# A fused attention and feed-forward kernel on one core: a new written-out instruction order and a constant tile set at the start

## The chip, the cores and the metric

One core of one Trainium2 chip runs the whole kernel; the other seven are idle. The metric is the device time of one execution in microseconds (us). The kernel before takes 803.41 us, the median of three runs (800.26, 803.41 and 803.42).

## What is computed

The reference runs three layers in a row. Attention has 2 batches, 8 heads, 768 positions and head size 64. Each position of q and k gets a 6-bit bucket from the signs of its product with `proj`, and a score counts only where the two buckets agree. Two feed-forward layers of 1536 tokens follow (512 to 2048 to 512):

```python
q_bits = (np.einsum('bhsd,dk->bhsk', q, proj) > 0)          # k_bits likewise
mask = q_bucket[:, :, :, None] == k_bucket[:, :, None, :]
scores = np.where(mask, scale * np.matmul(q, k.transpose(0, 1, 3, 2)), -1000000000.0)
attn = softmax(scores);  x = attn @ v
h = x @ w_in;   g = np.where(h >= 1, h, np.where(h <= -1, 0.0, (h + 1) ** 2 / 4));  x = g @ w_out
h = x @ w_in2;  g = h - np.tanh(h);                                                 return g @ w_out2
```

The four weight matrices arrive as 64-bit floats.

## The kernel before, in words

**Numbers as pairs.** TensorE multiplies in a format with fewer bits than float32, so each operand is kept as a high part and a low part (XH and XL, GH and GL, WH and WL, and so on), and a product is three matmuls: high by high, low by high, high by low. Making a pair takes a copy (`copy_hi`, line 235, the traced line is 236) on ScalarE or VectorE, and a subtraction (`sub_lo`, line 241), on GpSimd (traced as line 242) or VectorE (line 243).

**Attention.** A group is one head of one half of the query positions; it has three tiles of 128 queries, so there are 96 tiles. `prep_q`, `prep_k` and `first_k` make the pairs of q and k, and `q_bits` and `k_bits` multiply them by `proj` on TensorE and turn the signs into bucket rows on VectorE (lines 353 and 339). All results of these small products share the PSUM tile `pb`, and each of them must be read out by VectorE before the next is written. `emit_s` (lines 444 and 448) makes the scores of one tile; `soft` takes the maximum on VectorE (462), two small scalar steps (465), the exponential on ScalarE (466), and the high and low parts of the result (471 on ScalarE or VectorE, 472 on GpSimd or 473 on VectorE), which a transposing DMA on SP's queue turns around (477). `scale_l` prepares the division by the row sums (495, 499, 503) and `pv` multiplies by v (559). For three of the 16 pairs of heads `turn` transposes on TensorE instead (521, 529). `clear` (300 on ScalarE, 301 on GpSimd) writes zeros into the lower half of a pair's tile by scaling the identity matrix `unit`, which a DMA brings at the start.

**Feed-forward.** There are 128 units of 24 matmuls (`mats`, line 718), in six phases; a unit reads one or two blocks of weights. `w_narrow` turns a block of 64-bit weights into 32-bit ones (671 on ScalarE, 672, 673 and 675 on VectorE) and stores them for the second batch (679); `w_split` makes the pair. `post` evaluates the activation and adds up the outputs (737 to 768). The units of the first batch run between the attention tiles of the second half.

**Order.** Nothing loops on the chip. Python lists all steps as ops (`Plan.op`) with the cells they read and write, and a string, `SCHEDULE` (line 21), holds the order of the ops and, for each op that can run on more than one engine, which one runs it. `Plan.unpack` (line 96) reads it: three bytes an op, two for the place in the list of ops that are left, one for the engine. If the length does not fit or an op would come ahead of one that it depends on, the list's own order is used. Each engine then runs its ops strictly in the order of the string.

**The start and the spins.** Ahead of the ops a few lines are written out by hand (194 to 211). SP loads `proj` and the identity; VectorE sets constants, makes the pairs of `proj`, and at last copies the identity into `warm`:

```python
V.tensor_copy(warm, unit)        # line 211
def spin():                      # line 870
    for _ in range(4):
        T.matmul(WT, warm, warm, start=True, stop=True)
```

A spin is an op on TensorE whose product nobody reads; it keeps that engine active. There are 65, and the string places them like any other op (traced as line 872).

Of the kernel before, what the change touches and what calls it, by code (L numbers as in the profile page):

```python
# [20 lines left out]
SCHEDULE = (
    "c-rk)du)~E8GoMl@_p}jJKt%0F70VgdwMx-Y3cn!OE0ug5Gr+omWhs=8X&=V8JSClfCY3S0y+ehh{z=%x|<l83mGhIUXW-ci+51mqDz*|%s-4-X5yZ=OvQ5A"
    "o{Gub#uF&t_kPd&d!P6BT+9Bd90gV>x-OWe2@vFr#Xn<~qmCnhR7%{z{n{HG8^RW-L@ijVQUMq+&JIRou@3>BU+^hkJ-07D9UuT6WM{jPZp9dz)e3il!2<yh"
    "83hH^uJ9{Yun<7mzI{r6XN84^<M_Vs1QH3bqlotWP$2@&$;izOBId;7aaxPTY)8t>o4*r=o}Not8CfOq@3XGEzN4dKVjE&_?>f#;{{fgWsgW_Lt7~m-Mc@*q"
    "Pj{Okc6>^sgI!&dZ2NFW?ZS?ZB<p6ZxYJ~%rG>1eZX%Q*vb?;VERkD_<MTQ?V~IrKfxNsYlgVTwNpe+QUNP2K5FM``h(x2Mxhhmv7A`8TsK^e73Mwi9GPAO>"
    "jDn(!!t7`~uc9IzhlmL|;v>w=$a8rt*9l~2_XQm%9F9i&v$E=)42Ex1(k92U=w}w@x1Y!?b<i{&6_4BIZ*4QniXMrEVlhPHW8a8IeI{HXcrfVNwryGQ_>?ne"
    "EdIwGisz6#q!i$L_?mnbgBcL^*~=$gFXO|%y+R~gZ?acR&s)CSgTuJeF~PV(04TM@&+&6qL@6l^i%AJ^?X|A^){U&d;hY=HFhE|5NY5)dUjfk7)djatBEZR$"
    "+izTd@+6b+^2u%y3^p%byqG9#U~J*SmDmVN8Wz<!;BrUVSMJ%f2iR;@MreJ;Lq^|a;?!0#bITU-TKugzz$O8c5$`*Op4V~59UdOTyYBoI;<}b2M>x-{LX=Xj"
    "z*`k+`RVdqyK;B!`aYmxh+T*~$TY<Gb=yAsbQ@#$-pi0JWD5|lfx8gruEl4c?OgN0@7EkZj<TO__q*WpE4aV?*TC4}qel-NIz+MZ$tU>C$4@_f@F1E`y+`5y"
    "bMw@xQ<Ma6zWM(9^0C)Xp8;X-6K}t5oqhv|_m=?R#Yn_7Eel^faUu-cbjn2hc&?C+6h~DKDZnA)kRXN+W@cvUAP)rQ1p>kS-bdi?Wgoy_A@HXU{~QR|XPE1{"  # L30
    "?^^Ht<un6$=N-$+ef9MmMG_95)G#jzMybP}fBw1W=naoaOCAxXiI#yB-CRok6ylTOAD;jo#)C*{<Ue*G7Xtf%zV6xm>~8QLeRMYkC+!x(aLzc5_rrZe=w^95"
    "BSUg6C%|4?bhoy0m9cK6kq59{=r;yiwrtpdLOikqF%Y=>7Jn<-!q_7ZGQgia*ua-kfEcUxY^F?<13MY4-GNH2+I|~jLP~bk5BYL=i{#=a0es`300}`YUAh!)"
    "JH##P`u<6rlTT@P-=%g~R72JepthE{G+WEs$|jU`bSweUC?`xPSt!+P@||R?it;RmVTyy2l9J}4A|VoWbqgj>ork<8zp075dZiO1l~{6IcCA}p3=Sj`Av=*^"
    "mZ4^{DGdz`<SV0HAZBsiEPY>c^lOr?D+>w=cp@R}{5+v}EXIxcY{Ljs_yZk9>i_h^H8o*_gay4owc|JuKr1tcBg+lyWx9xA-b%H>3}RM<laZz=4Bw}kima}V"
    "g;{9s)mMjTqbj!z&N7ONi$O#a32AYF$=#V(vRG$lEY^-~Z3+XX5o!tv$C2Q(X+PsrNe4KY-rm)fB)=Cq%~au}EC>c!?W|3;m)`@>-{1dZ`b%kS2WHG*P=-!V"
    "k}6&Iwr<<^(Yp5rEo|8`p%{NsDWj=rpz-!KYvjPdfa}h;Ec@8ry)|IDa_7#Sp10!#Rd#H)G!+yd6^DPbY}w(WBLA7f!mS&*vGEtb^gO(4{S)gYP$Fd9!4&K?"
    "O$qKSd|Zgj_8&Ol;QsxTE(YAfmQi35L&z870si83_wQpbIGTq|KVrti*Wj(F>AU~n0Kk0|XzYm<_dE`Uv3}paBS#Q*HYmB{=>hYm?GKTF4X}bj33u-{_U_%h"
    "2XU9s!VLa!MDpzqz?Q8Bad2=mhmD)~#>Wo0F6Vo75wsXvvj*m55lLJ75w9o#^a~el*Z>K{e4TCv7^_!Xt5%uUOQ3{Ygp9ff;_4f5<ysGkriM9l=-u#5#7o&a"
    "A$oiFUL8b!8yGuKu&%DlIYh1r%nVSiW#}yV?riE(j?=ebK+c~(b0I7MF>fAxZ#uUxxp~@6jBz2J5X{b?;%WExavpBw^UNM#Qc)r^bN1}nbkP<eS}m(_#tcd%"
    "-v_9v!EPRbO4i;UV&$b&^_!Yd^HiV~m=rv1s@!NX?XE7PsS~lm1SAk4FYzRZDFPK1heDainp;|^Y*WxSH1MFy@-&6i!AgTc%d!k3zc!zc6|WeNszS%N@orKx"  # L40
    "c!^RxKR;jPR&`fZRiVX<aZ%Q&zt@3PSSZL@o|lD5CmZedcBYsMhHZP<*@lN)@XQ3EQ#24ZwF8zV1ic56fdVTiAQ;Ta<GF?riA0!b(w`upSpvl#_higLD;i}H"
    "A}O35iAE?Xi<6iMMMa6i5-N?Eh}0*YsOLDLZW0s-En21%5`!sIgqYSXdW7gi;=QA<5682K6QQrUrM$dsI>RokM*(x%IIq-o6(*F%lA@-jCI;k}Zq8xc`1bC("
    "6<2k6lPD<MmbU&30P<43UvE#HTCgY($elWM>a?oySJ`$&0Ooi!(EzwDI;?m@b#;sy#w5`tI{G@L%n~I+%qRw)&;_`oqq?)5SG85wRBQTpcek#B)zx)1t#k#Y"
    "nwxujVMe7nYgR$IoK}liJwsH{MLIhxD+N-C6{4i0zP_!^s&8!QYv}3esh?t5qPniWd$5cnwO%#}O6%&dzP`4$xwNT<^ZMq(!rF$)Lb_RFV>x5V(sAP|N-J5i"
    "jNquSl5=VHDJm%`Dk2QY;sv?%Au4i2gx<p<6eeMM?g-JS1G+a4W{?lmIvvX~4Bc}mEU3X{WVo(DvlulB(Ag}Id$!GV){=3=02KpG1kG#G)!E7{0@TIB(%(!$"
    "v{)8c)WNh!jlrq5Q)MM3WCmlNNA1D3IS*2^Wzw}AKx!|v?oq2mi&Gk!z-gaj(jFjSQs%_7<4~Xx9N{uWElKGSSn9s)lCeVgf;tzTEirl&0ZJi7wOyfQnFK)S"
    "O#4f5gZd9CNQ!8#1f?qXv~Mi*=xU6eJ&qdzs)S^nMPPJ_UZ>Vf&-5VlqYxCZlI}!LwoMELwHGx%N_SktJ&UCqj@~p#1_!F%Heph5GuoneGr^g5%b+$Htn&>}"
    "aBZSQZ8Br}j&u*&55&7pMj>eq^E?2?Q87<2NuDBikSQiLQK1Vr&5D{Gx~WJ00>LfXpok-ChBOh9S2;BWQ=6;D4#L;#WGvH7k*Yl%sSP7Ck%Jsm5lYgEkUC_@"
    "L?rHw!H^<Fb8rUKgPsXOPd4PF!Mx&{Uoq$%jZMVRJzz8$T|+CmUvuMdn?~8}4B6y3qiZ_p13Kp{IFKGfdImcwQJgVj<9P`7P!*lH`k$d+aAaIeL(?8%-G*;S"
    "Fs&t^Tpkv{N(*3YR^bq=&(rS9g`xI+Ge=uzk%nC9-?=@ys1%Q*?)?H?Y2CrMa}HFW|4?73oU1-8yc)rJ1^*?2-%_mqU6%e&DZD5b<)U1ai;{jTz_Vj4p1Uwq"  # L50
    "Ww@4s7jW*-BhuB!Zv|`Lm>HPHy>KLj)T4je<{^&FSvZQd_%$w%7Z^-<!It2EG?p&ZFg*X4tP4E_$7~1=4OdLZ*wI4jJS-d&Rp&qt8|XL|X3qJQ7Dr<WhfDBt"
    ">j$O?;xv;B$3z6CwKQB(A*B63A*r33DkyN&YBFkgUT~79wg5+De8?XBx(Ped)o^4yOqU8AbDv4Y0)EBGX&#vtA7h*>5XS0x9M$(@F1~5xXUcR&Oh1Nk4D$fu"
    "Xm`aiR{IeygNUii;dxfzuo;G5@gt@#Bg2*yOi_w)7{f8eOf+1d#MI8ik#jAT8*sEhfK;}BN#RgSQ*iMW=2K#g+QH6Wz+pmhxL${&x8AfS%nOr$0b~5bO#"
)


# [868 lines left out]
```

## Time and profile before

| | us |
|---|---|
| median of three runs | 803.41 |
| the profiled execution, own time | 806.18 |
| the profiled execution, span from first to last instruction | 804.4 |
| busy: TensorE matmul / VectorE / ScalarE / GpSimd | 755.5 / 607.2 / 461.8 / 307.5 |

The profiled execution is 2.77 us over the median, and 1.78 us of its time lie outside its span. A row of the trace names the engine (PE is TensorE's matmul, DVE VectorE, ACT ScalarE, POOL GpSimd, SPq SyncE's queue of DMA issues), the line, the operation, output<-inputs, shape and count. Square brackets hold the engine's idle time just ahead and what ended it.

### The profile page before, as it was taken

How to read it: one execution, taken by the hardware profiler on the slowest of the kernel's cores; microseconds unless marked ns; L12 is line 12 of the kernel's file. 1: busy time of each engine (PE TensorE's matmuls, PEld its weight loads, DVE VectorE, ACT ScalarE, POOL GpSimd, SP SyncE). 2: the span in 40 equal slices, each digit the busy share in tenths (PEclk: the TensorE clock that was granted, in tenths of full speed). 3: DMA queues.
4: the chain of work that ended last, by engine and by line, in shares of the span. 5: the costliest groups of instructions: out<-in, count | busy, mean ns of one | idle time of the engine just before them, and what ended most of it. 6: DMA issues, size and time to landing. Idle time of an engine off the chain costs nothing. (4 is left out here: it accounts for less than half of the span.)

```text
span 804.4 us, 12604 instructions
## 1 busy us (share of the span) xinstructions
PE 755.5 (94%) x4604; PEld 694.8 (86%) x4604; DVE 607.2 (75%) x1038; ACT 461.8 (57%) x747; POOL 307.5 (38%) x209
## 2 busy tenths in 40 slices
PE   5678999898899999998999999999999999999998
PEld 3557777777698899997999999989999999999997
DVE  7889988989898999999999998945444454444633
ACT  6778987977785778766865674524334132231220
POOL 6553254256444355533232554313131144202331
PEclk9999999999999999999999999999999999999999
DMA  5788696799967799397787788563221302121312
GB/s 183 144 197 207 178 233 184 205 227 240 210 182 179 187 220 225 108 215 208 195 201 215 194 193 206 160 137 125 66 66 53 92 27 79 59 74 52 92 40 79
DMA packets 163726, 123.38 MB, mean 153 GB/s; under 512 B 126800, under 2 KB 133712, under 8 KB 163664
## 3 DMA queue, kind: packets, MB, share of 16 engines
q1 hardware_dynamic: 163664, 122.58, 59.7%
q8 instruction: 36, 0.59, 0.3%
q14 instruction: 26, 0.21, 0.1%
HBM read 71.96 MB, written 19.92 MB: 114 GB/s over the span
## 5 line engine op out<-in xcount | busy, mean ns | idle before, releaser
L242 POOL TENSOR_TENSOR wl<-wr,wh 128x512 fp32r<-128x512 f32 x87 | 119.0, 1372 | 253.7 <-ACT wh L236 151.3
L718 PE MATMUL mm<-xh,wh 128*128 128x384 f32 x512 | 137.5, 339 | 2.3 <-DVE tmp L739 1.3
L718 PE MATMUL mm<-gh,wh 128*128 128x384 f32 x512 | 137.1, 338 | 2.1 <-DVE tmp L739 1.6
L718 PE MATMUL mm<-xh,wl 128*128 128x384 f32 x512 | 136.0, 336 | 0.4 <-POOL wl L242 0.4
L718 PE MATMUL mm<-gh,wl 128*128 128x384 f32 x512 | 135.6, 335 | 0.1
L718 PE MATMUL mm<-gl,wh 128*128 128x384 f32 x512 | 135.6, 335 | 0.1
L718 PE MATMUL mm<-xl,wh 128*128 128x384 f32 x512 | 135.6, 335 | 0.0
L472 POOL TENSOR_TENSOR phl<-p,phl 128x768 f16<-128x768 f32 x46 | 79.1, 1719 | 89.5 <-ACT phl L471 73.5
L236 ACT ACTIVATE wh<-wr 128x512 fp32r<-128x512 f32 x98 | 60.7, 623 | 83.5 <-PE mm L718 70.7
L466 ACT ACTIVATE p<-ss,sm 128x768 f32<-128x768 f32 x78 | 77.2, 990 | 47.0 <-DVE sm L465 46.1
L718 PEld LDWEIGHTS mm<-xh,wh 128*128 128x128 f32 x512 | 92.5, 189 | 5.4 <-DVE tmp L739 2.0
L718 PEld LDWEIGHTS mm<-gh,wh 128*128 128x128 f32 x512 | 92.4, 188 | 5.3 <-DVE tmp L739 2.3
L718 PEld LDWEIGHTS mm<-xh,wl 128*128 128x128 f32 x512 | 93.2, 188 | 1.0 <-POOL wl L242 0.7
L718 PEld LDWEIGHTS mm<-gh,wl 128*128 128x128 f32 x512 | 93.0, 188 | 0.8 <-DVE wl L243 0.7
L718 PEld LDWEIGHTS mm<-gl,wh 128*128 128x128 f32 x512 | 92.8, 188 | 0.7 <-DVE gl L243 0.6
L718 PEld LDWEIGHTS mm<-xl,wh 128*128 128x128 f32 x512 | 93.3, 188 | 0.0
L462 DVE TENSOR_REDUCE sm<-ss 128x1 f32<-128x768 f32 x82 | 78.1, 953 | 7.2 <-PE ss L448 6.0
L768 DVE TENSOR_TENSOR accs<-mm,accs 128x768 f32<-128x768 f32 x45 | 42.9, 953 | 36.1 <-PE mm L718 35.9
L242 POOL TENSOR_TENSOR gl<-tmp,gh 128x768 fp32r<-128x768 f32 x18 | 35.5, 1969 | 72.5 <-ACT gh L236 31.4
L471 ACT ACTIVATE phl<-p 128x768 f16<-128x768 f32 x65 | 54.6, 840 | 4.0 <-DMA pt<-phl 1.3
L243 DVE TENSOR_TENSOR gl<-tmp,gh 128x768 fp32r<-128x768 f32 x46 | 47.0, 1024 | 9.1 <-ACT gh L236 8.6
L671 ACT ACTIVATE w<-w 128x512 f32<-128x512 f32 x60 | 40.2, 670 | 23.2 <-DMA w<-in_w 23.0
(180 smaller groups left out, 1270.3 us busy)
## 6 DMA issues: line engine op xcount, KB each, us to landing
w<-in_w SPq DMA_DIRECT2D x60, 512.0 KB, 4.2
qr<-in_qT SPq DMA_DIRECT2D x32, 192.0 KB, 3.7
wr<-scr0i SPq DMA_DIRECT2D x24, 256.0 KB, 3.0
wr<-scr0o SPq DMA_DIRECT2D x24, 256.0 KB, 2.9
krs<-in_kT SPq DMA_DIRECT2D x14, 384.0 KB, 3.6
vr<-in_v SPq DMA_DIRECT2D x12, 384.0 KB, 4.0
scr0i<-wr SPq DMA_DIRECT2D x16, 256.0 KB, 3.7
scr0o<-wr SPq DMA_DIRECT2D x16, 256.0 KB, 3.0
```

The source lines that it names most:

```text
L236: ways = [("A", ca, lambda: A.activation(dst, src, AF.Copy)), ("V", cv, lambda: V.tensor_copy(dst, src), 1)]
L242: op([("G", cg, lambda: G.tensor_tensor(dst, src, hi.bitcast(F32), op=ALU.subtract)), ("V", cv, lambda: V.tensor_tensor(dst, src, hi.bitca ...
L243: ("V", cv, lambda: V.tensor_tensor(dst, src, hi.bitcast(F32), op=ALU.subtract), 1)], reads, writes)
L462: one("V", 870.0, lambda: V.tensor_reduce(z[:, 0:1], s, axis=AX.XY, op=ALU.max), cell, [c])
L466: one("A", 970.0, lambda: A.activation(halves(p), s, AF.Exp, bias=z[:, 2:3], scale=z[:, 1:2], accum_out=LS[lm][:, lk:lk + 1]), cell + [c], ...
L471: hi = [("A", 730.0, lambda: A.activation(hl[:, 0:S], p, AF.Copy)), ("V", 470.0, lambda: V.tensor_copy(hl[:, 0:S], p), 1)]
L472: lo = [("G", 1600.0, lambda: G.tensor_tensor(hl[:, S:2 * S], p, hl[:, 0:S], op=ALU.subtract)), ("V", 870.0, lambda: V.tensor_tensor(hl[:, ...
L671: one("A", 560.0, lambda: A.activation(y, y, AF.Copy, scale=2.0**-112), [], xc)
L718: T.matmul(ps[:, s + hf, 0:SH], m[:, kc * 128:(kc + 1) * 128], y[:, hf * SH:(hf + 1) * SH], start=(kc == 0 and i == 0), stop=(kc == 3 and ...
L768: one("V", 870.0, lambda: V.tensor_tensor(a, ps, a, op=ALU.add), [pc], c)
```

## The change

Two edits. The string is replaced, with 64 spins where there were 65. `warm` is no longer copied from the identity at the end of the opening lines; VectorE's first instruction sets all of it to 1.0.

```diff
-SPINS = 65
+SPINS = 64
 SCHEDULE = (
...
     SP.dma_start(out=pr_raw, in_=projR)
     SP.dma_start(out=unit, in_=eye)
+    V.memset(warm, 1.0)
     V.memset(half_b, 0.5)
...
     V.tensor_copy(phl_w[64:128], pl[64:128].bitcast(F32))
-
-    V.tensor_copy(warm, unit)
```

The new string holds 9,825 bytes, three for each of 3,275 ops, the old one 9,828 for 3,276; in both every op stands behind those it depends on. Apart from the spin the ops are the same. Read out, the two strings compare as follows (ops, not instructions):

| | TensorE | VectorE | ScalarE | GpSimd | SP |
|---|---|---|---|---|---|
| before | 1041 | 1023 | 650 | 205 | 357 |
| after | 1040 | 1004 | 664 | 210 | 357 |
| up to tile 59's maximum (VectorE) or exponential (ScalarE): before, after | | 447, 443 | 296, 297 | | |
| up to tile 95's: before, after | | 849, 838 | 544, 555 | | |

252 of the 862 ops with a choice of engine change engines, most of them in both directions. The largest nets: the high parts of q (line 275) go from 7 on VectorE to 2; the low part of the softmax result from 23 on VectorE and 55 on GpSimd to 18 and 60; the high part of weights from 46 on VectorE to 42. Of the other ops the order changes locally: half of them stand within 8 places of where they stood in the whole list, none moves by more than 248. The DMAs are the same ones on the same queue, in another order here and there.

The places that the prediction speaks of:

- TensorE's queue begins with five spins, where it began with one.
- The zeros of the first key tile (`bk` of group 0) were GpSimd's second op, behind one other clear; they are now ScalarE's fourth, behind three clears of 768 columns.
- On SP's queue the load of q for group 0 is issued between the two halves of its key's load; it came behind both.
- Ahead of `emit_s` of tile 35 TensorE has five steps of unit 4 (three matmuls each) where it had three behind the scores of tile 34; ahead of `scale_l` of tile 59 it has four steps of unit 18 (six matmuls each) where it had three.
- Between the two halves of `k_bits` of group 25 stood five steps of `pv`; now three steps of units 32 and 33 (six matmuls each) stand there, and the five of `pv` come behind. On VectorE the first half's read-out now has the first of its followers, `w_narrow` of block 52 and one subtraction, ahead of the second.

## Rows read from the trace of the kernel before

**Rows 1.** The head of the page: span, and busy time of each engine.

```profile
span 804.4 us, 12604 instructions
PE 755.5 (94%) x4604; PEld 694.8 (86%) x4604; DVE 607.2 (75%) x1038; ACT 461.8 (57%) x747; POOL 307.5 (38%) x209
```

**Rows 2.** Stretch, its length; busy (count) PE, PEld, DVE, ACT, POOL; clock; DMA; GB/s.

```profile
0.00:40.00 40.00, 24.76 (x90) 18.59 (x90) 31.82 (x67) 29.19 (x47) 24.55 (x19) 0.96 0.66 162
40.00:280.00 240.00, 215.54 (x1455) 177.76 (x1456) 216.98 (x419) 189.11 (x326) 108.04 (x72) 0.99 0.83 202
280.00:520.00 240.00, 235.23 (x1431) 220.78 (x1431) 224.74 (x377) 163.94 (x267) 100.19 (x67) 0.99 0.78 194
520.00:800.00 280.00, 279.51 (x1630) 277.54 (x1630) 132.67 (x176) 79.51 (x108) 74.69 (x51) 1.00 0.25 74
80.00:120.00 40.00, 38.76 (x262) 30.02 (x259) 35.84 (x73) 36.05 (x64) 15.95 (x11) 1.00 0.84 207
```

**Rows 3.** Groups of instructions, shapes apart: the spins.

```profile
L872 PE MATMUL pb<-warm 128*128 128x128 f16 x260 | 22.8, 228 | 14.2 <-DVE warm L211 5.6 <-DVE bq L353 2.3 <-DVE gl L339 1.6
```

**Rows 4.** Timeline of TensorE at the start: start us, us, what.

```profile
5.63 0.61 PE L872 MATMUL pb<-warm 128*128 128x128 f16 x4 [5.63 <-DVE warm L211]
...
7.91 0.69 PE L319 MATMUL pb<-bk,pw 128*128 128x384 f32 x1 [1.24 <-POOL bk L301]
```

**Rows 5.** Timeline of VectorE at the start.

```profile
0.81 0.06 DVE L196 MEMSET cb<- 128x1 f32 x1 [0.81 <-PEq L917]
...
2.64 0.24 DVE L203 TENSOR_SCALAR tmp<-tmp 128x6 f32<-128x6 f32 x2 [1.31 <-DMA tmp<-in_proj]
...
4.80 0.77 DVE L211 CAST warm<-unit 128x128 f16<-128x128 f32 x1
```

**Rows 6.** Timeline of ScalarE at the start: a clear, and the first load's end.

```profile
3.31 0.93 ACT L300 ACTIVATE bq<-unit 64x384 fp32r<-64x384 f32 x2 [1.29 <-DMA unit<-in_eye]
4.70 0.94 ACT L236 ACTIVATE ak<-krs 128x384 fp32r<-128x384 f32 x2 [0.46 <-DMA krs<-in_kT]
...
7.96 0.84 ACT L300 ACTIVATE gl<-unit 64x768 fp32r<-64x768 f32 x1
```

**Rows 7.** Timeline of GpSimd at the start.

```profile
5.55 2.30 POOL L301 TENSOR_SCALAR bk<-unit 64x768 fp32r<-64x768 f32 x1
```

**Rows 8.** Timeline of TensorE, waits at 142 and 272 us.

```profile
142.32 0.61 PE L444 MATMUL ss<-xh,aq 128*128 128x384 f32 x2 [2.47 <-ACT p L466]
...
272.87 0.38 PE L499 MATMUL pb<-unit,rb 128*128 128x128 f32 x1 [1.48 <-ACT rb L495]
```

**Rows 9.** Timeline of TensorE around 365 us.

```profile
360.41 2.63 PE L559 MATMUL pv<-pt,v 128*64 128x384 f16 x30
365.72 0.44 PE L335 MATMUL pb<-ak,pw 128*128 128x384 f32 x1 [2.68 <-DVE bk L339]
```

**Rows 10.** Timeline of VectorE in the same stretch.

```profile
361.22 2.02 DVE L673 SCALAR_TENSOR_TENSOR wr<-w,wr 128x512 int32<-128x512 int32 x1
...
363.33 1.44 DVE L243 TENSOR_TENSOR aq<-qr,aq 64x384 fp32r<-64x384 f32 x1
...
365.05 0.61 DVE L339 TENSOR_SCALAR bk<-pb,cb 12x384 fp32r<-12x384 f32 x1
```

**Rows 11.** One stretch of 5 us, columns as in group 2.

```profile
365.00:370.00 5.00, 3.90 (x12) 3.59 (x13) 4.64 (x7) 3.79 (x6) 0.31 (x1) 0.67 0.09 29
```

**Rows 12.** Groups of instructions, shapes apart: subtractions on VectorE and GpSimd.

```profile
L243 DVE TENSOR_TENSOR bk<-krs,ak 64x768 fp32r<-64x768 f32 x4 | 3.8, 947 | 0.0
L243 DVE TENSOR_TENSOR xl<-krs,xh 64x768 fp32r<-64x768 f32 x2 | 3.9, 1937 | 0.0
L473 DVE TENSOR_TENSOR phl<-p,phl 128x768 f16<-128x768 f32 x23 | 24.0, 1047 | 0.8 <-ACT phl L471 0.7
L472 POOL TENSOR_TENSOR phl<-p,phl 128x768 f16<-128x768 f32 x46 | 79.1, 1719 | 89.5 <-ACT phl L471 73.5 <-DVE phl L471 3.8 <-issue 3.4
```

**Rows 13.** Waits of TensorE: who for whom, us, times, longest.

```profile
PE pv L559 <- DMA pt<-phl: 0.2, 1, 0.2
```

More of the change, by code (lines that the diff above doesn't have):

```diff
@@ L17 @@
 AX = mybir.AxisListType
-SPINS = 65
+SPINS = 64
 SCHEDULE = (
[L22 to L53, printed above, removed]
@@ new lines @@
+    "c-rk)d5l%%6+h=&@4eq$-ZuMVX5KKvykYjmVPJG--V8Gg%YZs9o8X%2*eY(-ST))}6+}@{A_zznMRBR3R{yX{EYWHtm}qJ=HBsAQYOLuWwux=jq~|`O0<!~}"
+    "{=o^%+<U*}obx;9{LX>S^|dS3t&6TT`QSLKLF)GaVp^jBj{{z*Es1Dx4$~uz62L#-12-PGjj_+s)!Kr=e27FMAYneti$t*4Kv6}0f!EguoR{R3=d@}ak3*x@"
+    "jFpy_di79=)dp`UbDV;BJf16r$-nf9vNDTBr%h{a-n`kKf<aM{Rmj0XEaeDOrZ9*OM*n^N6hy}@fY0auBXPzVc|zC+`}%Zm<f9B@^VvM+53uzT+S^5UA1TkY"
+    "4!SOXm3QuQG-4YfIHI?=YPLv&)}5UfXx-5<+bQD@mpxROelYsLX)p~MR57&HLMoNKn^iTj;)XhaWPbiF>8h&2)%k60MHLklmX(*+kW+6pL1SJ`A~D@cB+AMX"
@@ new lines @@
+    "smAJtsnZixsp{&IM9hxGVkyXn+PspIa!99hgPgLWsVVLkeD3>x(vJs0USVO<kHkGMFE3V5Q0bL>!uO+Y>_9BGUkH&(Iox>rxJjiFI+aT4{Cq1G7n<Uty$Hl)"
+    "dHJV&w=o9~9)uuptR03G78bIP9LK@;Wc2-bemoCBx?B*(XMp{N7y0EY-X9<u^}o6MWnK1r^dYWdSA#J|O4kK&^u==M+M!1~nCJTdt}DY8i)qFBSNBU`fQ*R`"
+    "p|g|o(@s0BJBN3@bLrdHah^%E?H`I=L`I8dY;7Gn=Nx|a*&LSC*MsLhvSQaR3gh&r1_#*=#@IHH@*%ldBJZEad0%qN+wb*lAdxaHIe(o_c<cAQ#$Ih-w~k3E"
+    "S4*}g`Xpm%I{NIRmZTJV>Vs>Ix#B8wrBZkqZrQPAi~iz^&6_vN#YzhK*@Z&u3pU<yhp^rkZ*4dr)PAM-8}Rymk^_v{Drfbtl~OM$^5(i1U;cXU-e+GHzF;rB"
@@ new lines @@
+    ";CTcFd`vPE;3>=c6#o9#Pd<49?ol8A<sdEY`T&u?Z_I%M2AwzGME;iHs9uFPw6-;<y?Y5mN7y!MeI8?Zd61h+$t@`HzJB7X2>vIw8+`v?;73dleDMXqmtSU;"
+    "Y5n2foR0}_^#R2q|J^@Vz`MFE_fHytuqp(2Q|`|Rg246|bDVwq99!EqfB6-qU*z!0H*n=wQvUaMl;T_nczVyCe?IffZ`o&r7w1J#RJb!{+xCMycZS%zih{^F"
+    "xxaB^La7?QAxa?n8wqIGP_}!G&=%eEG^Lolf72%1x)p)%R0>$+vh8#^zsp11gn0Met1i3{ezA%%3mSIOZoL{21%n$<T_*&^;_9uW=Gt6R6vr65{PN4;f-reV"
+    "as|^mhH8M;nCDXBA==ffm({bn40G9nOQwri<>e~`D~3|W&V`zq2B=Qf)h($@{&Z<AVr5lj<*Zq=Dl4lmAeUNT8d9w+TUJI)5pZ5vNi<cl#26-1b66=LF-~bk"
@@ new lines @@
+    "c`21eb5T=M6ZucXrtEq<9*YUi>(aHg#nb97M5W49syt<;B%P##$(ouD3jwF(N=OTlFB+o_B_)yC+8pvUh<XLYc*!JT5_dT-c7nn}C@wAzw3W*ejJd83tSH#6"
+    "t*W{@8YK_w>gu#yER~{j)2fJKDG1K|`IH<<J%x<pidaR@YUj|}I%CERN!%NqJ2%?k`$6Ex2`kkTKzUae&Kw$ow)?o8H49446#!~*kf5)vwFU+T&KNlT^cu?o"
+    "b0efHuZLJHI(xR=)dlxh6anO`(45Ld;n2|9wYT1SD_Bn$adY!;Tz6$tllyLCqj>n8hYi^n1affu_U%e<bt_$d-@WB~FPZn!JzJtt%c3lV+xPgy3x+-Z_~R?r"
+    "?T$Ed7Z1cu&pr42^IAXGawd4ED|NM@N>IwWGZLX{)I%3<dukgz>GCy?ao0ZorkfrTJMR))y|m-D+X#0RJg>6p%DeXLv0V4D*O+D5yLa36BWu}<>>;{=>1UqN"
@@ new lines @@
+    "tG3^GpOUtC^2zI@e(W)=H)`!@ZPsr~?s(t<pyb+2+Fsy_Z``zr>aK*{c_(w|=CuW9-At^#bm`Lj@5d$T*NZ9X@h-&JU5pKEz;lu-lk3(Y7E%(-z6pMIM^A2n"
+    "{VNIQ-EuprK1;4$3v{{fFNQ&5$V%qv1!u3kYR#IWd8n2_J_FTrK3sFnHSWFlN_lqPO2=8{I4j(_b3s^Cd~A_1iv|p5^Ui|h%gwT7_6iisBb@)7L=fR&SQyaf"
+    "=oQhZ-K;Z<1Mmk~R~PH-yhi#97oL7|uEhQYoHsZ3_Y;Fhb-bg4Q7uC{PWJG@-ri<r+dzE{mTO`X*PS-4rKLqFW6DB<tNW|9=4svCZStkn(IL12CN0Y%&5n~>"
+    "kC{wCcQ+SZXh+iNc3IAOjN;<t5O{`hpq!e;CAlI~%|R*W9@a7=v8o{Li$8jv;-U#DehR7A#KW3~*i@337SsnpsocQJwzO1=J5H4A=H|HH2vF|^0s1~eYM~|Q"
@@ new lines @@
+    "Oo>DSDoz?90_vYm6->3uD$2~%xF4N4v$)MFPBrkr^HQlgB4d!$iW5#^;lhNoNS08qGJSobudhhVW?;HJFGnv}uz(72Zgc@9BkPA2vWr6|Q-5j@h?+Ak*6+?a"
+    "rLT`G$1Cq8{+Zg4X@s*VZ!Bw}Wiet3oHJ)mef?D4bWu<PIXTNSnPgff5{U|LDr;_bTcRxyfZpETX!6{KXmtAY4nG!KvSbMW^$(I(Q_|AH=W&}xrQU+UhMpeN"
+    "tE)0y&H$usno!y+D`yL9v5=Cv;?zZp+84HWkVa|*#>|;vSZAh_RSkq<has)4?VIrv@`;&wrn`HNub1|BWjv4is@>g@ncbb~=urLrjx+aEHM55rco(#UWti&e"
+    "ncE{}TU%R)=T*12a^6DpIfJpbQ<~bs>}-Mt#;V%uWHsfFZb=K2kP;O&gl|bI1(YZyDOn1H9h8(1`z4^Tkn<dX94{xxP2><G#^WaLClZ8MD70b#>`-Wa1RXwz"
@@ new lines @@
+    "Fwdp3ga(a<o;@xlAwwe~r_gcw9rh6+c=i~&mH~QmsWVYSrBg(a+_EHfcuHF!_N0CiN=S`7tbNi!)b4VcQ-Jt`BA5*Vacf8c)SoRHVF~MyT4nZH>Y~EX8Lh$="
+    "Cs=3)9j794ke*FQN#WE(kKtK*rYa5RD?3aMMzctGkK$wly^xEc2bx)meo_e#5+S^yi4aa%h7cqNsB9gF4AaE@G)HhQDd%afbsTNeQrP3k;_TSqkXxGCF1kR2"
+    "OL&*hsJa;vNQ%otM$%3)E5tDiipX+F7E83Vpz=e|S>c{6T-ksS7F0zv9*QjB9$~`iuL$P@@|5w=H*S$FbR8O{C=A4pq?KHBL%bvtJk%w4_6&_e#NuHjgvAeO"
+    "pl{?C1xjn5f=N_EEE>KM0QA+NZQLUNRA?GG%nqq#A{(;MR-{mp4<VM^4l@fvU&Fa5eBj8#eaN#bWHf>9hLdafljP9P!(`kK?)MMF_I|(aj{9LeJ?8rdbHpbD"
@@ new lines @@
+    "ql+1P`P<vf(YwsBmvOE+UO6$>J4gLKBzWWp9Q{0wxq3{doRIza-5wm(zzG@t?I!#C?e;iF?1|q>HI?OZ`*?t}57%iAH{pmE>)Stve>w8QWW^fk%{pA6HOi6i"
+    "EU}JBr!}GhKe!;Al>ZOGlMy^AC*`D^l#_CNjU+pXjnx|PM`;{*LNCCv#@|tIK>Xp&9DO1_aaiGaA;aUh7f+<~c=VMxuDLkAKX~HO4=1y0QrdBx_~S8HkE3fj"
+    "{?Oq>UBU?`{BU%~SQ|YQ_(LS^xQcPYalkRr!NY*T$)(Q3fWYDQ;5Y|y;wTNveVm}NlP;{unmi7djKdu`Y98T;r8}}cI58fZOkcnWJdAh`!sLyCNoLxQ@lVcC"
+    "7+?Yc#tAplqf&R=U=62>V~1c8bT&p4nONE3*mQd2e|C=2OpdnUyZXT4=WrBez%ehz(Y!sJeh^2aZycu!92V!pO+_4&#c<?Fa-_RPOr#^-$B{GdyQVRAqK!Dr"
@@ L54 @@
+    ";%G^NBUv!A;iEw{437~H;js+46PN!1Aq&t>"
 )
```

## The prediction

> **What bounds the kernel now.** I read the head of the page first: TensorE's matmuls are busy 755.5 of 804.4 us, every other engine less [rows 1]. So the end is set by TensorE's work plus the time in which it has none, and only the second can shrink here, since the change leaves TensorE's ops alone but for one spin. That second part is 48.9 us idle (804.4 - 755.5) and, inside the busy time, 22.8 us of spins, which fill holes [rows 3].
>
> The view by stretches says where the holes are [rows 2]. From 520 us on TensorE is busy 279.51 of 280 us; nothing that the order does there can help, and only a mistake could hurt. From 280 to 520 us it idles 4.8 us, from 40 to 280 us 24.5 us, in the first 40 us 15.2 us. So the change must earn its gain ahead of 280 us, with a little up to 520. Who makes TensorE wait there? VectorE is busy 216.98 of 240 us from 40 to 280 (90%), ScalarE 79%, GpSimd 45% [rows 2]. VectorE is near its limit, and because each engine runs its ops strictly in the order written, one late op delays all behind it.
>
> How long the last part is, is settled too: behind the last tile's scores both orders have the same steps of TensorE. The time is thus "when the last tile's scores are done" plus a constant, and a hole closed ahead of that is worth its full length only if no later one opens.
>
> **The change part by part.**
>
> *The memset.* `warm` is set by one VectorE instruction at about 0.81 us in place of the copy at 4.80 [rows 5]. A memset of one column takes 0.06 us, the copy of all 128 took 0.77; the new one lies between. VectorE then has 1.31 us of idle time ahead of its first use of `proj`, which waits for a DMA [rows 5], so the memset costs nothing; without that cover it would cost at most 0.77. The copy's slot (4.80 to about 5.25) goes to a copy of half a key, which ScalarE did before, as soon as the load lands at 4.70 [rows 6]: no gain of its own.
>
> *Five spins first.* They can run from about 1.1 us instead of 5.63 [rows 4]. Nothing useful on TensorE is ready before about 6 us, so the spins themselves bring nothing: 0, unless they raise its clock earlier. The first product of 384 columns takes 0.69 us at 7.91 [rows 4] and two in a row 0.61 at 142 [rows 8], so the start does run slow; but five spins are followed by some 3 us of nothing, and I count no gain. The far end: all matmuls of the first 28 us at the full rate, perhaps 3 us off a chain that is partly waits; I keep that for the range.
>
> *The zeros of the first key.* The first product that needs them waits until 7.91 for GpSimd [rows 4], whose clear ran from 5.55 to 7.85 [rows 7]. Now it is ScalarE's fourth clear of 768 columns. ScalarE's first clear starts at 3.31, when the identity has landed, and one of 768 takes 0.84 [rows 6]: 3.31 + 4 x 0.84 = 6.67, so 1.2 us earlier. What is queued behind on ScalarE are two more clears and the copy of the key's second half, so that half comes later than before; the q load that is now issued ahead of that half on SP's queue is one DMA and hidden by those clears. Ends: 0 (the second half, or the next key's load, takes over) and -2.4 (the read-outs behind gain as much again). I take **-1.2**, the one length that rows give.
>
> *VectorE's load ahead of 280 us.* Up to the maximum of tile 59, which lies at about 265 us, VectorE has 443 ops in place of 447. In the first 280 us its mean is (31.82 + 216.98) / (67 + 419) = 0.51 us an instruction [rows 2], so 2.0 us less, on an engine that is 90% busy: **-1.8**. ScalarE has one op more there (on an engine with 21% to spare: nothing), GpSimd as many as before, and SP the same DMAs. The ends are 0, if ScalarE or a chain of waits paces this stretch, and -2.0. Ahead of the last tile VectorE has 11 fewer, but in that part TensorE is at 98% (235.23 of 240), so the other seven bring nothing beyond the holes counted next.
>
> *More work ahead of known waits.* At 142 us TensorE idled 2.47 us for the exponential that frees the score tile of tile 35 [rows 8]; two more steps of three matmuls now stand ahead of it. At 272 us it idled 1.48 us for the row sums of tile 59; one more step of six does. In the full stretch 1,630 matmuls take 280 us, 0.172 each [rows 2], so either place gets 6 x 0.172 = 1.03 us more to do: **-2.1** together. Ends: 0, where the moved steps wait themselves, and -3.95, both waits gone.
>
> *The wait at 365 us.* Five steps of `pv` cover the read-out of the first half of `k_bits`, and then TensorE idles 2.68 us [rows 9], because VectorE reaches that read-out only at 365.05: ahead of it a shift of weights took 2.02 us and a subtraction 1.44 [rows 10]. Now 18 matmuls (3.1 us) stand between the halves and `pv` behind. 3.1 us are more than the 2.68 idle, but the 2.6 us of `pv` no longer lie there; VectorE's slow instructions, though, have moved too. I take the whole wait, **-2.7**. Ends: +1.0, if the read-out stays where it is in VectorE's queue and the next wait (the read-out of unit 32) is late instead, and -4.35: after the wait the granted clock in this stretch is 0.67 of full [rows 11], a fall to the lower level (1.2 GHz) for about 3.3 of the 5 us, which costs another 1.65.
>
> *Engine choices.* Five more low parts of the softmax result go to GpSimd: 1.719 us there for 1.047 on VectorE [rows 12], 0.67 us later each at the transposing DMA. They hide: TensorE waited for such a DMA once, for 0.2 us [rows 13]. If that cover were gone they would cost 5 x 0.67 = 3.4.
>
> One behaviour speaks against moving work to GpSimd. A subtraction on VectorE of the same shape took 0.947 us in four cases and 1.937 in two [rows 12]. The row does not say why. The Trainium skill ("SBUF — State Buffer", "Who interferes with whom") says that a VectorE instruction with two SBUF inputs and a GpSimd instruction that reads SBUF exclude one another, the second one waiting out the first. By that rule alone (an estimate) each of the five could hold VectorE up for as long as it lasts, 5 x 1.719 = 8.6 us, and the sum would come out near zero. The trace agrees with the direction: 1.0 us more for a subtraction. I price it as a rival.
>
> *The sum.* -1.2 - 1.8 - 2.1 - 2.7 = -7.8 us, the removed spin 0. Against the profiled execution's own 806.18 that is 798.4. That execution is 2.77 over the median; taken off the median, 803.41 - 7.8 = **795.6**.
>
> **The rivals.** A measurement of this kernel can tell about 0.5% from no change, 4.0 us: faster is under 799.4, slower over 807.4.
>
> *A, the sum as above:* 795.6. For it: three holes that I can point to, with more work ahead of each. Against it: it takes them as independent.
>
> *B, the holes only move:* VectorE and ScalarE pace the first 280 us, their loads hardly change, and what is closed at one wait opens at the next. Then only the start and the load remain: 803.41 - 1.2 - 1.8 = 800.4, no change. For it: VectorE's 90%. Against: the best 40 us of that stretch have 1.24 us of idle time where the mean is 4.1 [rows 2], at a VectorE load as high (35.84).
>
> *C, GpSimd holds VectorE up:* the five low parts that moved each cost their 0.67 us and one blocked subtraction, 1.0 us [rows 12]: +8.4, and with the 3.0 us of B left, 803.41 - 3.0 + 8.4 = 808.8, slower. It decides once the transposed results come late enough that `pv` waits for them, or once VectorE's blocked time lies ahead of a read-out of `pb`. Against it: the 0.2 us of that wait [rows 13], and as many GpSimd ops up to tile 59 as before.
>
> *D, the order is better throughout:* if half of the way from the mean of the stretch from 40 to 280 us to its best 40 us is gained, the idle 24.5 us shrink by (24.5 - 6 x 1.24) / 2 = 8.5 in place of the 2.1 counted: 795.6 - 6.4 = 789.2. Nothing but the wholesale reordering speaks for it.
>
> That the string is not used at all is excluded: its length fits and its order is a valid one.
>
> **How the numbers follow.** A 0.50, B 0.28, C 0.14, D 0.08. Faster is A and D, 0.58; no change B, 0.28; slower C, 0.14. The range from 788 to 805 takes in D, A and B with the ends of their terms (B at its worst adds 1.0 at 365 us and the 3.4 of uncovered transposes: 804.8) and leaves out C and the far side of D, together under 0.2. A's own range is 791 to 799.
>
> **What would show it.** The first spin at about 1.1 us; the first product with `bk` at about 6.7 in place of 7.91; VectorE with 1,019 instructions, ScalarE 761, GpSimd 214, TensorE 4,600. Idle time of TensorE from 40 to 280 us near 20 us; no wait of over 1 us at the second half of group 25's `k_bits`, and a granted clock of 1.00 there. Rival B shows as the same idle time with other waits on top; C as subtractions on VectorE with a larger mean, and TensorE's `pv` waiting for DMAs. The prediction is wrong if TensorE's idle time ahead of 520 us does not fall, or if new idle time appears behind 520.

## The result and the profile after

The changed kernel takes **792.66 us** (median of five runs, 791.67 to 794.25) against 801.59 for the kernel before in the runs taken with it: ratio **0.9893**, interval 0.9865 to 0.9920, that is 8.6 us less (6.4 to 10.8). Forecast were 795.6 us, 7.8 us less. On another chip the same pair gave 0.9895. So the size was right. The experiments below show that this is in part luck: two terms of the sum bring nothing, and another is several times too small.

The head of the page of the changed kernel, beside [rows 1]:

```profile
span 789.9 us, 12622 instructions
PE 748.6 (95%) x4600; PEld 691.4 (88%) x4600; DVE 597.3 (76%) x1019; ACT 465.2 (59%) x761; POOL 314.0 (40%) x214
```

The instruction counts are the forecast ones. TensorE idles 41.3 us (789.9 - 748.6), where it idled 48.9. The view by stretches (stretch, its length, busy time and count of PE, PEld, DVE, ACT and POOL, granted clock, DMA share, GB/s), beside [rows 2]:

```profile
0.00:40.00 40.00, 27.25 (x162) 21.63 (x162) 34.82 (x79) 32.21 (x54) 25.08 (x22) 0.96 0.79 187
40.00:280.00 240.00, 220.41 (x1463) 183.32 (x1464) 218.21 (x421) 193.84 (x337) 114.36 (x76) 0.99 0.82 208
280.00:520.00 240.00, 235.14 (x1445) 222.12 (x1445) 221.95 (x364) 159.79 (x267) 102.25 (x68) 1.00 0.78 198
520.00:785.00 265.00, 264.81 (x1532) 263.73 (x1529) 121.35 (x154) 79.34 (x105) 72.34 (x49) 1.00 0.22 67
```

From 40 to 280 us TensorE idles 19.6 us where it idled 24.5; from 280 to 520 us 4.9, as before (4.8). Not only the idle time fell: TensorE is also busy 6.9 us less (755.5 to 748.6), with four matmuls fewer. To see where the lead arises, the table follows one event through the profiled executions: the start of the n-th tile's second score step (the n-th pair of rows of TensorE's line 448), in us from the span's start.

| score pair | 1st | 7th | 13th | 19th | 25th | 37th | 61st | 79th | 96th | span |
|---|---|---|---|---|---|---|---|---|---|---|
| before | 14.5 | 33.2 | 51.1 | 72.7 | 92.3 | 147.3 | 268.8 | 394.2 | 520.4 | 804.4 |
| changed | 13.8 | 29.6 | 46.1 | 63.3 | 81.3 | 134.1 | 257.5 | 382.8 | 506.2 | 789.9 |
| lead | 0.7 | 3.6 | 5.0 | 9.4 | 11.0 | 13.2 | 11.3 | 11.4 | 14.2 | 14.5 |

The two profiled executions differ by more than the medians do (14.5 against 8.9 us, as the one of before lies high among its runs), so the shape counts here: 11.0 of the 14.5 us are there at 92 us, in the stage in which TensorE has attention alone. Another pair of executions (f1 and experiment 8, below, on other chips) has a lead of 12.0 us there, of which 7.3 are left at the end. The kernel before and then the changed one up to that event, the start of their 25th score pair, in the view by stretches:

```profile
0.00:92.30 92.30, 69.98 (x420) 51.58 (x421) 79.55 (x167) 71.34 (x125) 44.89 (x34) 0.96 0.72 181
```

```profile
0.00:81.30 81.30, 64.78 (x440) 48.99 (x441) 71.68 (x160) 67.43 (x117) 46.53 (x38) 0.98 0.80 202
```

Up to the same event VectorE has 7 instructions fewer and works 7.9 us less, ScalarE 3.9, TensorE 5.2; GpSimd has 4 instructions more. VectorE's idle time falls too, from 12.8 to 9.6 us. So most of the early lead goes with a smaller load on VectorE ahead of these tiles, and the rest with less waiting.

### The profile page after: what moved, and what is told of

The parts are those of the page before. It is cut to its first block, busy times and chain, and to the rows that moved or that the text cites. A ratio compares the mean times of both kernels' runs of the same rounds, so it can differ in the third digit from the quotient of the medians.

```text
span 789.9 us, 12622 instructions
## 1 busy us (share of the span) xinstructions
PE 748.6 (95%) x4600; PEld 691.4 (88%) x4600; DVE 597.3 (76%) x1019; ACT 465.2 (59%) x761; POOL 314.0 (40%) x214
## 4 chain that ended last, share of the span: by engine, by line
PE 60%; DVE 8%; ACT 3%; issue 1%; DMA 0%; DVEq 0%; ACTq 0%
PE mm L718 54%; PE pv L559 2%; DVE gl L243 1%; PE ss L444 1%; PE ss L448 1%; DVE wl L243 1%; DVE phl L473 1%; DVE sm L462 1%; DVE tmp L742 1%; DVE wr L673 1%; PE pb L499 1%; DMA w<-in_w 0%; ACT gh L236 0%; DVE wr L672 0%; ACT w L671 0%
## 5 line engine op out<-in xcount | busy, mean ns | idle before, releaser
L472 POOL TENSOR_TENSOR phl<-p,phl 128x768 f16<-128x768 f32 x51 | 90.7, 1779 | 90.2 <-ACT phl L471 75.1
L236 ACT ACTIVATE wh<-wr 128x512 fp32r<-128x512 f32 x102 | 63.3, 623 | 77.4 <-PE mm L718 70.0
L243 DVE TENSOR_TENSOR gl<-tmp,gh 128x768 fp32r<-128x768 f32 x49 | 56.4, 1156 | 5.0 <-ACT gh L236 4.7
L741 ACT ACTIVATE tmp<-mm 128x768 f32<-128x768 f32 x32 | 26.0, 811 | 53.5 <-PE mm L718 39.4
L739 DVE SCALAR_TENSOR_TENSOR tmp<-tmp,mm 128x768 f32<-128x768 f32 x32 | 30.5, 952 | 35.2 <-ACT tmp L738 35.0
```

What stands on the lines that cost most here:

```text
L236: ways = [("A", ca, lambda: A.activation(dst, src, AF.Copy)), ("V", cv, lambda: V.tensor_copy(dst, src), 1)]
L243: ("V", cv, lambda: V.tensor_tensor(dst, src, hi.bitcast(F32), op=ALU.subtract), 1)], reads, writes)
L472: lo = [("G", 1600.0, lambda: G.tensor_tensor(hl[:, S:2 * S], p, hl[:, 0:S], op=ALU.subtract)), ("V", 870.0, lambda: V.tensor_tensor(hl[:, ...
L739: one("V", 870.0, lambda: V.scalar_tensor_tensor(halves(t), halves(t), 1.0, ps, op0=ALU.min, op1=ALU.max), [pc], [c])
L741: one("A", 690.0, lambda: A.activation(halves(t), ps, AF.Tanh), [pc], [c])
```

## The experiments

Each ran in five rounds beside the kernel before (the seventh in three). Where the string changes, the diff says how it was put together. Ratios are to the kernel before, in brackets the interval. All of these kernels do the whole of the reference's work; only order, engines, spins and the way `warm` is set differ.

**1. The early spins alone.** The old order, with four more spins at the head and the memset.

```diff
-SPINS = 65
+SPINS = 69
-SCHEDULE: old
+SCHEDULE: four spins, then the old order; old engines
+    V.memset(warm, 1.0)
-    V.tensor_copy(warm, unit)
```

> The kernel before with the memset and with four more spins at the head of TensorE's queue (69 in all), so that it begins with five as the changed kernel does; order and engines are the old ones. Theory ORDER (the gain is the new order and engine choices): 0 within 0.3%, ratio 0.997 to 1.003. Theory CLOCK (the gain is that TensorE's clock rises at 14.7 us in place of 28.8, because spins run from 1.05 us): the clock rises before 20 us and the ratio is 0.993 to 0.996, 3 to 5 us, which is what stands between the two kernels at the scores of tile 9.

Measured: 0.9978 (0.9953 to 1.0002), 1.8 us less, and none lies within the interval; at most 3.8 us are what the early spins give in the old order. Its matmuls do go over to the full rate earlier: a product of 384 columns takes 0.66 us at 17.17 and 0.34 at 19.55, where the kernel before went over at about 29. But the granted clock (1.00 is the higher level, 2.4 GHz, 0.50 the lower, 1.2 GHz) of its profiled execution falls again behind that. Experiment 1 and then the changed kernel from 25 to 40 us:

```profile
25.00:40.00 15.00, 11.44 (x46) 9.23 (x44) 12.67 (x30) 12.59 (x23) 8.65 (x5) 0.66 1.13 199
```

```profile
25.00:40.00 15.00, 11.45 (x74) 9.35 (x73) 14.17 (x36) 12.87 (x23) 9.17 (x7) 0.89 1.13 211
```

So the run does not bound what an early clock that stays is worth in the new order.

**2. The new string without the memset.**

```diff
-    V.memset(warm, 1.0)
     V.tensor_copy(phl_w[64:128], pl[64:128].bitcast(F32))
+    V.tensor_copy(warm, unit)
```

> The changed kernel with warm copied from the identity as the last of the opening lines, as before; the new string with its five spins first stays. Theory ORDER: the spins move to about 5.3 us and end near 7.5, one us behind where the first product started (6.48), so at most +1.5 us on the changed kernel: ratio to before 0.989 to 0.992. Theory CLOCK: the clock rises late again and 3 to 5 us are given back: ratio 0.994 to 0.996.

Measured: 0.9858 (0.9831 to 0.9886). The five spins now come late and push the first product back, from 6.48 to 8.37 us, as its timeline of TensorE shows:

```profile
6.30 2.31 PE L873 MATMUL pb<-warm 128*128 128x128 f16 x20 [6.30 <-DVE warm L212]
8.37 0.67 PE L319 MATMUL pb<-ak,pw 128*128 128x384 f32 x1
```

No loss can be told from none in the end: the interval overlaps that of the changed kernel. So the memset gives nothing that these runs can tell, and the string alone gives the change.

**3 and 7. Order and engines crossed.** The new order with the old engines, and the old order with the new ones.

```diff
-SCHEDULE: new order, new engines
+SCHEDULE: new order, old engines     # 3, on the changed kernel
-SCHEDULE: old order, old engines
+SCHEDULE: old order, new engines     # 7, on the kernel before
```

> The changed kernel's order and memset with the old engine for each of the 252 ops that changed engines. If the order alone carries the gain: ratio 0.988 to 0.993. If order and engines only work together, because each place was chosen for an engine: 0.997 to 1.01, as VectorE then has its 19 ops more and some stand at the head of a queue that they were not placed for.

> The kernel before with the new engine for each of the 252 ops that changed engines, in the old order and with the old copy to warm. If moving 19 ops off VectorE is worth something by itself: 0.992 to 0.997. If order and engines only work together, as the opposite pairing showed (1.092): 1.03 to 1.10.

Measured: **1.0918** (1.0886 to 1.0950) and **1.1149** (1.1103 to 1.1196). Each half of the string alone costs 74 to 92 us. Experiment 3 from 40 to 280 us, against the changed kernel's row above:

```profile
40.00:280.00 240.00, 202.71 (x1314) 163.72 (x1312) 208.66 (x386) 175.45 (x304) 101.62 (x68) 0.96 0.76 190
```

Every engine is less busy there than in the changed kernel: TensorE falls from 220 to 203 us, VectorE from 218 to 209, ScalarE from 194 to 175, GpSimd from 114 to 102. Over the whole run VectorE works 29.7 us more (627.0 for 597.3), ScalarE and GpSimd some 7 us less each (458.7 for 465.2, 307.1 for 314.0), and the span is 88.3 us longer. Of these, 61.4 us are idle time of TensorE (102.7 for 41.3) and 26.9 busy time (775.5 for 748.6, at a granted clock of 0.96 for 0.99 in the row above). The idle time goes into waits that did not exist before. The first lines of TensorE's waits (who for whom, us in total, times, longest):

```profile
PE ss L449 <- ACT p L471: 10.2, 13, 1.8
PE mm L723 <- DVE wl L248: 10.2, 6, 3.6
PE mm L723 <- POOL wl L247: 8.2, 6, 3.4
```

A weight's low part that comes late from either engine stops a whole unit. In these two strings, a place in a queue is only good for the engine that it was chosen for.

**4 and 5. The string cut at tile 17.** New up to the exponential of tile 17 and then old, and the other way round.

```diff
+SCHEDULE: first 350 entries of the new string, then all other ops as in the old one   # 4, on the changed kernel
+SCHEDULE: first 341 entries of the old string, then all other ops as in the new one   # 5, on the changed kernel
```

> The new string up to the exponential of tile 17 (the first 350 entries, 30 spins among them), and from there the old order and the old engines of all ops that are left (65 spins in all). Theory FIRST STAGE (the 9 us that the traces show at the scores of tile 18 are kept to the end): ratio 0.987 to 0.991, and the 5 us that the profiled executions differ further on are mostly noise between executions. Rival THROUGHOUT (the rest has its own part): 0.992 to 0.996. Rival PACED (VectorE's load ahead of tile 59 sets the pace, and an early lead is eaten up): 0.997 to 1.0.

> The old string up to the exponential of tile 17 (341 entries, 18 spins among them), then the new order and engines for all that is left (64 spins, with the memset). The other half of the run that took the new string up to tile 17 only (ratio 0.993). Theory THROUGHOUT (both halves have their own part and add up to the full change, 0.986 on that chip): 0.991 to 0.995. Rival FIRST STAGE: 0.997 to 1.0.

Measured: 0.9928 (0.9902 to 0.9954) and 0.9956 (0.9931 to 0.9981). The product, 0.9884, is the whole change. About 60% of the gain (5.8 of 9.3 us; by the interval 3.7 to 7.9) is made in the first 70 us or so, the start with its spins and zeros among them, and kept to the end; the rest has its own part. Experiment 4 keeps its lead: its 25th score pair is 5.5 us ahead of the kernel before (86.8), its 96th 5.1 (515.3). Its early lead is thus not eaten up further on.

**8. The three waits alone.** The kernel before, with TensorE's queue changed at the three places that the prediction priced.

```diff
+two steps of unit 4 ahead of emit_s of tile 35
+one step of unit 18 ahead of scale_l of tile 59
+three steps of units 32 and 33 between the halves of k_bits of group 25; the five of pv behind the second
```

> The kernel before with TensorE's queue changed at three places only, as the new string has them: two more steps of unit 4 ahead of the scores of tile 35, one more step of unit 18 ahead of the product of tile 59's row sums, and three steps of units 32 and 33 between the halves of group 25's k_bits, with the five steps of pv behind the second half. Theory SUM (each hole closed ahead of 520 us is gained): the three terms of the prediction, -2.1 and -2.7, so ratio 0.993 to 0.996. Rival MOVE (a hole closed here opens at the next wait): 0.998 to 1.002.

Measured: **1.0000** (0.9975 to 1.0025). The waits do shrink or move. Rows of its timeline of TensorE, beside [rows 8, 9]:

```profile
142.89 0.62 PE L449 MATMUL ss<-xh,aq 128*128 128x384 f32 x2 [1.38 <-ACT p L471]
...
359.57 0.44 PE L340 MATMUL pb<-ak,pw 128*128 128x384 f32 x1 [2.44 <-DVE bq L358]
...
364.72 0.34 PE L340 MATMUL pb<-ak,pw 128*128 128x384 f32 x1
```

At tile 35 the wait falls from 2.47 to 1.38 us, as the two added steps should make it (1.03), but the score starts at 142.89, no earlier than the 142.32 of before: ScalarE's exponential sets that moment, and work pulled ahead of it only empties the queue behind. At the second half of `k_bits` (364.72) the wait of 2.68 us is gone, but the three steps between the halves came from ahead of the first half, and now that half stands 2.44 us (359.57) until VectorE has read out the product of `q_bits`: it does so at 358.90, where it did at 358.78 before, as VectorE's queue was left as it was. In the interval at most 2.0 of the 4.8 us can be hidden.

**6. No spins.** The changed kernel, and (**f3**) the kernel before, without any.

```diff
-SPINS = 64          # f3: 65
+SPINS = 0
-SCHEDULE: as it is
+SCHEDULE: as it is, the spins left out
```

> The changed kernel without any spin; all else as it is. If spins only fill holes and cost nothing: ratio to before 0.985 to 0.990, and a granted clock like that of the changed kernel. If they hold TensorE's clock up: the granted clock is at the lower level in longer stretches ahead of 200 us and the time is 1 to 2% longer than the changed kernel's, 1.0 to 1.01. If spins stand in the way (they share a tile with the small products and wait for its readers): 0.980 to 0.985.

> The kernel before without any spin, all else as it is. INTERLOCK: 3 to 6 us less, 0.992 to 0.997, as the new order without spins gained on the new order. Rival (the old order needs them for the clock): 1.0 to 1.008.

Measured: **0.9815** (0.9789 to 0.9842) for the new order, 0.9985 (0.9957 to 1.0013) for the old. Without spins the changed kernel gets faster again; the old one gets nothing that can be told from none. Experiment 6 by stretches:

```profile
0.00:40.00 40.00, 24.96 (x78) 18.58 (x78) 33.78 (x79) 31.89 (x54) 25.91 (x22) 0.89 0.77 190
40.00:280.00 240.00, 215.93 (x1315) 178.61 (x1315) 222.12 (x428) 195.00 (x339) 115.74 (x77) 0.98 0.85 211
```

The granted clock is 0.89 for 0.96 in the first 40 us and 0.98 for 0.99 behind, while VectorE does 222 us of work in the second stretch where it did 218. The figures for the first 40 us are too high: the view gives 1.00 from 10 to 15 us of the changed kernel, where two scores take 0.84 us that take 0.56 later.

The two kernels without spins also show the two orders at nearly the same clock. f3 and then experiment 6, up to the start of their 25th score pair:

```profile
0.00:86.40 86.40, 62.49 (x328) 44.22 (x329) 78.14 (x167) 71.16 (x125) 45.87 (x34) 0.94 0.75 193
```

```profile
0.00:79.90 79.90, 61.08 (x317) 44.35 (x318) 70.33 (x160) 67.19 (x117) 47.03 (x38) 0.94 0.79 203
```

The new order is 6.5 us ahead there, with the same 7 instructions fewer on VectorE and 7.8 us less of its work. So an early lead of that size needs no better clock. These are single executions, and that of f3 is the fastest of its twelve.

**f1, f2 and f6. What in a spin costs.** The changed kernel once more, on the chip of f2; the new order with eleven spins at the head of TensorE's queue and none behind; and the changed kernel with one matmul a spin.

```diff
-SPINS = 64
+SPINS = 11                                  # f2; SCHEDULE: eleven spins, then the new order without spins
-        for _ in range(4):
+        for _ in range(1):                  # f6
             T.matmul(WT, warm, warm, start=True, stop=True)
```

> The changed kernel as it is, on the same chip as the two runs below: 0.986 to 0.992.

> The changed kernel with spins at the head of TensorE's queue only: eleven (44 small matmuls, about 1.05 to 5.9 us, up to where the first product can start), none behind. Theory INTERLOCK (spins cost because they write a tile whose readers on VectorE then wait for them, and they for the readers; those at the head meet no reader): no worse than without any, 0.978 to 0.984 against 0.9815, and better by 1 to 3 us (0.978 to 0.981) if an early rise of the clock is worth something. Rival CLOCK (what spins cost is paid back by the clock): 0.984 to 0.990, as the changed kernel.

> The changed kernel with one matmul in each spin in place of four; the 64 spins stay at their places. Theory INTERLOCK (a spin costs by the waits between it and the readers of the tile it writes, whatever its length): most of the 7 us that spins cost stays, ratio 0.987 to 0.991. Theory LENGTH (a spin costs the time of its matmuls, which delay the useful step behind it): three quarters of the 7 us come back, 0.982 to 0.985.

Measured: f1 0.9895 (0.9871 to 0.9919), 795.74 us; f2 **0.9817** (0.9787 to 0.9847), **788.73 us**; f6 0.9852 (0.9822 to 0.9881). On one chip, the changed kernel with spins at its head alone is 7.0 us faster than as it was changed to, and its ratio is that of the kernel with none. Either version beats both kernels.

f6 lies just outside the range of LENGTH and below that of INTERLOCK, and its interval reaches into both: how much of the cost goes with the matmuls is not decided. Most of the waits stay. Who let the spins of the changed kernel run, from the view of line 872 (us, times):

```profile
its engine sat idle before it (us, times) until:
...
  DVE xl L339: 3.6, 5
  DVE bk L322: 3.2, 2
  DVE vsm L366: 2.8, 2
  DVE bq L353: 2.5, 3
...
who waited for it (us, times):
  DVE bq L353: 3.0, 3
```

And of f6, with a quarter of the matmuls:

```profile
  DVE xl L339: 3.8, 5
  DVE bk L322: 3.0, 2
```

A spin writes the unused columns of `pb`, the tile of the small products. VectorE's read-outs of that tile (339, 322, 353, 366) release the spins, and 353 waits for spins in turn, though nobody reads what they write. These rows show waits and not what they cost, as a spin may stand idle in a hole that would be there without it (TensorE idles 48.1 us in experiment 6, 41.3 in the changed kernel). How the 7.0 us divide between the length of the spins, these waits and work that they delay further on is open; spins that write a tile of their own were not run.

## Why the prediction was right, and where its steps were not

**The total.** -7.8 us forecast, -8.6 (6.4 to 10.8) measured, and rivals B (-3.0) and C (+5.4) lie outside the interval. D (-14.2) does too. But the total is in part luck, as the terms below miss in both directions.

**TensorE's work, held for fixed: wrong.** The prediction let only the 48.9 us of idle time shrink. In the profiled pair the idle time fell by 7.6 us and the busy time by 6.9. The same matmuls took less time, the scores above all, as fewer of them ran at the lower clock. First before, then changed:

```profile
L444 PE MATMUL mm<-ak,aq 128*128 128x384 f32 x8 | 3.5, 559 | 0.0
```

```profile
L444 PE MATMUL mm<-ak,aq 128*128 128x384 f32 x8 | 2.5, 400 | 0.0
```

How much of the 8.6 us that is, no run separates.

**The memset: right.** The row stands where it was expected, and VectorE's idle time ahead of `proj` covers it, beside [rows 5]:

```profile
0.83 0.17 DVE L197 MEMSET warm<- 128x128 f16 x1 [0.83 <-PEq L917]
...
2.75 0.24 DVE L205 TENSOR_SCALAR tmp<-tmp 128x6 f32<-128x6 f32 x2 [1.32 <-DMA tmp<-in_proj]
```

**The five spins: right within the bounds.** They start at 1.05 us. Experiment 1 gives 1.8 us for them in the old order, between the 0 that was taken and the 3 that was kept. The step that the prediction doubted did happen: the first product runs at the lower rate (0.69 us), and from 14.56 us on the matmuls follow one another twice as fast, where the kernel before reached that at about 29.

```profile
1.05 2.31 PE L872 MATMUL pb<-warm 128*128 128x128 f16 x20 [1.05 <-DVE cb L200]
6.48 0.69 PE L318 MATMUL pb<-ak,pw 128*128 128x384 f32 x1 [3.11 <-DVE ak L236]
7.16 0.66 PE L319 MATMUL pb<-bk,pw 128*128 128x384 f32 x1
...
12.45 0.84 PE L444 MATMUL ss<-ak,aq 128*128 128x384 f32 x2
...
14.56 0.56 PE L444 MATMUL mm<-ak,aq 128*128 128x384 f32 x2
```

The Trainium skill ("TensorE: Matmul & The Clock Gate", "Part 1: The HAM clock gate") says that the throttled state is the default and that activity releases it. These rows agree in kind (two scores take 0.84 us at 12.45 and 0.56 at 14.56). Experiment 2 shows that the rise comes just as early without an early start of the spins (by 14.5 us its matmuls are at the full rate too, with the spins at 6.30), so the memset is not needed for it.

**The zeros: right in kind, too long by 0.5 us.** ScalarE's clear ended at 6.15 us as 5.33 + 0.82, half a microsecond ahead of the forecast 6.67, but the product then waited for VectorE, whose copy of half a key took 0.98 us beside GpSimd's clears. The first product with `bk` is at 7.16 for 7.91, 0.75 earlier, and the first score pair 0.7.

```profile
5.33 0.82 ACT L300 ACTIVATE bk<-unit 64x768 fp32r<-64x768 f32 x1
```

**VectorE's load: right in kind, the size is the step that failed.** The prediction counted ops ahead of tile 59 (443 for 447) and multiplied by a mean, 0.51 us: -1.8. Up to the 61st score pair VectorE does have 4 instructions fewer, but it works 5.0 us less, before and then changed:

```profile
0.00:268.80 268.80, 230.58 (x1489) 187.10 (x1490) 237.87 (x468) 210.28 (x360) 127.20 (x89) 0.99 0.81 197
```

```profile
0.00:257.50 257.50, 225.16 (x1479) 184.25 (x1479) 232.91 (x464) 207.11 (x359) 127.08 (x90) 0.98 0.80 203
```

Up to the 25th pair it is 7.9 us, by the rows further up. There it is the subtractions of low parts (lines 243 and 473): 12 of them, 12.4 us, before, and 7, 5.4 us, after. The low parts of q, up to that pair, before and changed:

```profile
L243 DVE TENSOR_TENSOR aq<-qr,aq 64x384 fp32r<-64x384 f32 x4 | 2.2, 551 | 0.1
```

```profile
L243 DVE TENSOR_TENSOR aq<-qr,aq 64x384 fp32r<-64x384 f32 x1 | 0.6, 555 | 0.0
```

The two of 1.937 us [rows 12] have become three of 0.944. So the count was taken where much of the difference has been made up again, and a mean priced ops that are longer than it. Of the lead, 11.3 us are there at the 61st pair, 9.4 of them at the 19th. Experiment 4 fits: the first 350 entries alone give 5.8 us. That the load makes the lead is read from the traces, with f3 and experiment 6 as the second pair; no run changed the load alone, and experiment 7 shows that fewer VectorE ops in the wrong places cost far more than they save. How much the early clock adds, and which of the many small moves count, was not separated.

**The three waits: wrong as separate terms.** Closed alone they give 0 (experiment 8). In the changed kernel all three are gone:

```profile
129.88 0.50 PE L444 MATMUL ss<-xh,aq 128*128 128x384 f32 x2
...
262.01 0.83 PE L499 MATMUL pb<-unit,rb 128*128 128x128 f32 x6
...
351.84 0.34 PE L335 MATMUL pb<-ak,pw 128*128 128x384 f32 x1
```

but there others stand a little later, where before there was none over 0.4 us:

```profile
367.01 0.62 PE L718 MATMUL mm<-xh,wh 128*128 128x384 f32 x2 [0.90 <-DVE vsm L369]
...
374.07 0.62 PE L718 MATMUL mm<-gh,wh 128*128 128x384 f32 x2 [1.58 <-DVE tmp L742]
```

0.90 + 1.58 is nearly the 2.68 that went, and the idle time from 280 to 520 us did not fall. The first half of `k_bits` does not stand here as it did in experiment 8: it runs at 348.33, and VectorE starts its read-out of `q_bits` at 347.59. The prediction's own rival B had this mechanism; it priced it for the whole change when it held for these terms. What the new order does keep is the clock: 1.00 where [rows 11] had 0.67, and 1.00 too from 345 to 355 us, where its `k_bits` of group 25 lie.

```profile
365.00:370.00 5.00, 4.10 (x24) 3.78 (x23) 4.72 (x13) 3.58 (x5) 0.00 (x0) 1.00 0.73 199
```

**Engine choices: priced as small, right only together with the order.** The prediction took order and engines as two sums to be added. Experiments 3 and 7 show that neither has a worth of its own. The right question was not "how many instructions fewer" but "is each still in time".

**GpSimd against VectorE (rival C).** The subtractions on VectorE did get longer in some groups. First the kernel before, then the changed one, subtractions of 128x768:

```profile
L243 DVE TENSOR_TENSOR gl<-tmp,gh 128x768 fp32r<-128x768 f32 x46 | 47.0, 1024 | 9.1 <-ACT gh L236 8.6
```

```profile
L243 DVE TENSOR_TENSOR gl<-tmp,gh 128x768 fp32r<-128x768 f32 x49 | 56.4, 1156 | 5.0 <-ACT gh L236 4.7
L473 DVE TENSOR_TENSOR phl<-p,phl 128x768 f16<-128x768 f32 x18 | 20.2, 1121 | 0.2 <-ACT phl L471 0.2
```

1.156 for 1.024 us and 1.121 for 1.047 are some 8 us of VectorE's time in all (49 x 0.132 + 18 x 0.074). The Trainium skill ("SBUF — State Buffer", "Who interferes with whom") says that a VectorE instruction with two SBUF inputs and a GpSimd instruction that reads SBUF contend. The trace agrees in direction; no run here shows that GpSimd made them longer. TensorE waited little for it, 1.1 us in two waits where there was none before:

```profile
PE mm L718 <- DVE gl L243: 1.1, 2, 0.9
```

40 of the 49 run behind 280 us, where TensorE mostly has its work ready. Its `pv`, by which rival C was to show, waited for no transposing DMA.
